# Attention and two expert layers in one program: sums, inversion and division of the last two attention halves placed one to three expert steps later

## The chip, the core and the metric

The program runs on one core of a Trainium2 chip. The metric is the device time of one execution in microseconds (us); the time before is the median of three runs. TensorE is called PE here, its weight loads PEld, VectorE DVE, ScalarE ACT, GpSimd POOL, and SP is the engine whose queue issues nearly all DMAs.

## What is computed

A clustered attention (queries see only the keys of their own cluster) feeds two feed-forward layers; the second one ends with a product with a cosine.

```
mask = q_assign[:, :, :, None] == k_assign[:, :, None, :]
scores = np.where(mask, scale * np.matmul(q, k.transpose(0, 1, 3, 2)), -1000000000.0)
attn = np.exp(scores - np.max(scores, axis=-1, keepdims=True))
attn = attn / (np.sum(attn, axis=-1, keepdims=True) + 1e-09)
x = np.matmul(attn, v)            # batch 2, heads 8, tokens 768, head size 64
x = transpose(0, 2, 1, 3) of x, as 1536 tokens x 512
h = np.maximum(x @ w_in, 0.0);  x = h * h @ w_out        # 512 -> 2048 -> 512
h = x @ w_in2;  out = (h * np.cos(h)) @ w_out2           # 512 -> 2048 -> 512
```

All inputs and the output are float32. The matrix products of the two layers are made of three products of split operands (a high and a low part).

## The kernel before, in words

**Attention.** The 16 heads of the two batches are 8 pairs of heads. The 768 queries of a pair are two halves of 384, so there are 16 halves, numbered 0 to 15; the last two are 14 (`last`) and 15 (`end`). A half has six units of scores, one per 128 keys: `scores` (L454, PE into one of three two-bank `unit` tiles), `exponent` (L464, ACT), `add_up` (L476, POOL, which adds the six exponentials into `acc`), and `pv` (L484, PE, the product with v into `o_ps[0]`, three units at a time).

**What ends a half.** `move_out` (L535, ACT) copies the product out of `o_ps[0]`; `sums` (L499, eight small matmuls on PE) adds `acc` over the keys into the bank `o_ps[1]`; `move_sums` (L506, ACT) copies them out of it; `deal_sums` (L513, a DMA of SP) spreads them over 128 partitions; `invert` (L517, DVE) takes reciprocals; `store_inverse` (L523 or L525) and `load_inverse` (L531, two DMAs) bring them back as rows over 64 partitions each; `divide` (L538, DVE) multiplies; `combine_high` (L559, ACT) and `combine_low` (L563, POOL) write the result's high and low parts into `xh` and `xl`, the input of the first layer.

**Expert steps.** `moe` walks over steps 0, 1, 2, ...: a step is one block of 512 tokens and one group of 128 hidden units. Step i makes `h_mm(i)` (L674, twelve matmuls into one bank), then its elementwise work (`ew_first`: L689, L690, L691 on ACT; `ew_last`: L712, on POOL in the first steps), and `y_mm(i-2)` (L727, twelve matmuls). The banks of `h_mm` turn in a ring of four from step 2 on; two of the four are `o_ps[0]`, which step 3 takes, and `o_ps[1]`, which step 5 takes. Block 0 (steps 0 to 7) needs halves of the first batch only; steps 8 to 15 (block 1) read what half 14 writes, steps 16 on (block 2) what half 15 writes.

**Weights.** Each half of a weight group (`w_f_0` for `h_mm`, `w_f_1` for `y_mm`) is loaded by SP (`w_load`, L118) and split by `w_split`: six DVE instructions (L143, L144, L145, L146, L147, L139) and one cast on ACT (L138), which reads what L146 writes. `split_some` puts a share of these into each step. `load_mid` issues six such loads, `load_late` eight; the latter need the memory of the attention's tiles.

**What sets the order.** Every engine runs its instructions in the order in which the program writes them. During attention the order is a sorted list of due times (the tables `finish` and `places`); in the expert steps it is the text of `moe`, with hooks: functions that are called in step i right after `h_mm(i)`, before the elementwise work and the `y_mm` of that step. For half 14 `sums`, `move_sums`, `deal_sums` and `invert` stand in the table, and the rest in hooks 0 and 2; half 15 has all after `move_out` in hooks 3 and 5, with the division not dealt over partitions (its reciprocal works on `r` itself).

Of the kernel before, what the change touches and what calls it, by code (L numbers as in the profile page):

```python
# [38 lines left out]
def tile_kernel(ctx: ExitStack, tc: tile.TileContext, q, k, v, centroids, w1i, w1o, w2i, w2o, out):  # L39
# [69 lines left out]
    def w_load(m, f, hs=(0, 1)):  # L109
        wi, wo = ((w1i, w1o), (w2i, w2o))[m]  # L110
        for h in hs:
            raw_ = wraw[m, f, h] = chunk(f, h, U32, f"wraw{m}_")
            if h == 0:
                raw_ = raw_.rearrange("p (a c) -> p a c", a=KD)
                src = wi.bitcast(U32)[:, f * 2 * P : (f + 1) * 2 * P].rearrange("(a p) c -> p a c", p=P)
            else:
                src = wo.bitcast(U32)[f * P : (f + 1) * P, :]
            nc.sync.dma_start(raw_, src)  # L118
# [49 lines left out]
    NU = NPAIR * SP  # L168
# [8 lines left out]
    def small():  # L177
        return free_small.pop(0)

    def give_small(u):  # L180
        free_small.append(u)
# [259 lines left out]
    last = 2 * NPAIR - 2  # L441
# [25 lines left out]
    def add_up(u_):  # L467
        hb, kt = divmod(u_, NT)
        if kt == 0:
            return  # L470
        assert u_ not in unread and u_ - 1 not in unread
        if kt == 1:
            accs[hb] = ap.tile([P, 2, HALF], F32, tag="acc", name=f"acc{hb}", bufs=2)
        a = ptiles[u_ - 1] if kt == 1 else accs[hb]
        for j in range(2):
            nc.gpsimd.tensor_tensor(accs[hb][:, j], a[:, j], ptiles[u_][:, j], ALU.add)  # L476

    def pv(u_):
        n, c = divmod(u_, SP)
        hf, kt = divmod(c, NT)  # L480
        t = ptiles[u_]
        assert u_ not in unread
        for j in range(2):
            nc.tensor.matmul(  # L484
                o_ps[0][j * D : (j + 1) * D, :HALF], lhsT=raw[n, "v"][:, kt, j, :], rhs=t[:, j],
                start=(kt == 0), stop=(kt == NT - 1),
            )
# [5 lines left out]
    def sums(hb):  # L493
        su[hb] = u = small()
        a = accs.pop(hb)
        for j in range(2):
            for h in range(2):
                g = R * (2 * j + h)
                nc.tensor.matmul(  # L499
                    u[g : g + R, 0, :QH], lhsT=ones[:, :R], rhs=a[:, j, h * QH : (h + 1) * QH], start=True, stop=True  # L500
                )

    def move_sums(hb):
        u = su.pop(hb)
        r = inv[hb] = ap.tile([P, QH], F32, tag="r", name=f"r{hb}", bufs=2)
        nc.scalar.activation(r, u[:, 0, :QH], AF.Identity, bias=eps)  # L506
        give_small(u)


    def deal_sums(hb):  # L510
        r = inv.pop(hb)
        t = inv[hb] = ap.tile([P, 2 * HALF // P], F32, tag="dealt", name=f"dealt{hb}", bufs=2)
        nc.sync.dma_start(t, r[0:P:R])  # L513

    def invert(hb):
        r = inv[hb]
        nc.vector.reciprocal(r, r)  # L517

    def store_inverse(hb):
        r = inv.pop(hb)  # L520
        row = rows_[hb] = dram.tile([2, HALF], F32, tag="row", name=f"row{hb}", bufs=2)
        if r.shape[1] == QH:
            nc.sync.dma_start(row.rearrange("j (h c) -> (j h) c", h=2), r[0:P:R])  # L523
        else:
            nc.sync.dma_start(row.rearrange("j (a c) -> (j a) c", c=r.shape[1]), r)  # L525

    def load_inverse(hb):
        row = rows_.pop(hb)
        rb = rbs[hb] = ap.tile([P, HALF], F32, tag="rb", name=f"rb{hb}", bufs=2)
        for j in range(2):  # L530
            nc.sync.dma_start(rb[j * D : (j + 1) * D], row[j : j + 1, :].broadcast_to([D, HALF]))  # L531

    def move_out(hb):
        x = xs[hb] = ap.tile([P, HALF], F32, tag="x", name=f"x{hb}", bufs=3)
        nc.scalar.copy(x, o_ps[0][:, :HALF])  # L535

    def divide(hb):
        nc.vector.tensor_tensor(xs[hb], xs[hb], rbs.pop(hb), ALU.mult)  # L538

    def combine(hb):  # L540
        combine_high(hb)
        combine_low(hb)
# [14 lines left out]
    def combine_high(hb):  # L557
        for src, dst, low in parts_of(hb):
            nc.scalar.copy(dst, src)  # L559

    def combine_low(hb):
        for src, dst, low in parts_of(hb):
            nc.gpsimd.tensor_tensor(low, src, dst.bitcast(F32), ALU.subtract)  # L563
        xs.pop(hb)
# [248 lines left out]
    def load(m, f, h, at):  # L813
        w_load(m, f, (h,))
        ready[m, f, h] = at
# [19 lines left out]
    def moe(hooks):  # L835
        phs = {}
        for idx in range(n_steps + LAG):
            fresh = idx < n_steps
            yi = idx - LAG
            end = yi in closes  # L840
            for i in (idx, idx + 1) if idx == n_steps - 2 else (idx,):
                if i < n_steps and i not in phs:
                    phs[i] = h_mm(i)
                    loads_h(i)
                    if steps[i][0] == 1:
                        ew_zero(i, phs[i])
            for f in hooks.get(idx, ()):
                f()
            two = 0 <= idx - 1 < n_steps and steps[idx - 1][0] == 1
            if two:  # L850
                ew_mid(idx - 1, phs[idx - 1])
                by_pool = idx - 1 < n0 + 16
                if end or by_pool:
                    ew_last(idx - 1, nc.gpsimd if by_pool else nc.vector)
            if end:
                y_mm(yi)
                y_out(yi)
            if fresh:
                ew_first(idx, phs[idx])
                if steps[idx][0] == 0 and idx < FA:  # L860
                    ew_last(idx, nc.gpsimd)
            if two and not (end or by_pool):
                ew_last(idx - 1, nc.vector)
            split_some(idx, 12)
            if fresh and steps[idx][0] == 0 and idx >= FA:
                ew_last(idx, nc.vector)
            if yi >= 0:
                if not end:
                    y_mm(yi)
                loads_y(yi)  # L870
        assert not pending and not owed and not splitting
# [130 lines left out]
        (17.431, combine_high),  # L1002
        (18.530, combine_low),
    ]
    ending = sums, move_sums, deal_sums, invert, move_out

    SCORES, EXPS, SMAX, LARGEST = (0.000, -0.982, -0.808, -1.110, -3.572, -3.690), (0.016, -0.428, -0.788, -0.613, -3.224, -3.681), (-2.502, -5.046, -2.335, -1.548, -2.669, -0.447), (-0.170, -4.189, -2.105, -1.354, -2.566, 0.314)
    ADD, PV, WEIGHTS, WARMTH = 1.481, -1.548, 0.96, 0.97
# [31 lines left out]
        (pv, 89): 89.454, (move_out, 14): 89.482, (invert, 13): 89.676, (scores, 90): 90.000,  # L1040
        (exponent, 90): 90.016, (scores, 91): 90.018, (scores, 94): 90.428, (combine_low, 12): 90.531,
        (exponent, 91): 90.572, (exponent, 94): 90.776, (store_inverse, 13): 91.168, (scores, 92): 91.192,
        (exponent, 92): 91.212, (scores, 95): 91.310, (exponent, 95): 91.319, (sums, 14): 91.408,
        (move_sums, 14): 91.869, (scores, 93): 91.890, (load_inverse, 13): 92.298, (exponent, 93): 92.387,
        (pv, 90): 92.452, (pv, 91): 92.453, (pv, 92): 92.454, (divide, 13): 94.260,
        (deal_sums, 14): 94.761, (combine_high, 13): 95.431, (invert, 14): 95.676, (combine_low, 13): 96.531,
    }
    own_places = {key[0] for key in places}
    steps_ = []
# [1 line left out]
    def at(when, f, *a):  # L1051
        steps_.append((places.get((f, *a[-2:]) if f in own_places else None, when), len(steps_), f, a))
# [32 lines left out]
        for r, f in finish:  # L1085
            at(NT * hb + r, f, hb)
    for r, f in finish:
        if f in ending:
            at(NT * last + r, f, last)
    for g in range(-LEAD, NU):  # L1090
        c = g % len(SMAX)
# [30 lines left out]
    def load_late():  # L1122
        att.close()
        late = ctx.enter_context(tc.tile_pool(name="late", bufs=1, reuse_waits="tile"))
        for f, h in wanted[n_early + n_mid :]:
            home[f, h] = late, f"l{f}_{h}"
            if (f, h) not in STAGE:
                load(0, f, h, 6)

    open_banks()  # L1130
    end = last + 1
    moe({
        0: [lambda: store_inverse(last), lambda: load_inverse(last)],
        1: [
            lambda: add_up(NU - 3), lambda: add_up(NU - 2),
            *(lambda u_=u_: pv(u_) for u_ in range(NU - GROUP, NU)), lambda: move_out(end),
        ],
        2: [
            lambda: add_up(NU - 1), lambda: divide(last), lambda: combine(last), load_mid,
        ],  # L1140
        3: [
            lambda: sums(end), lambda: move_sums(end), lambda: invert(end),
            lambda: store_inverse(end), lambda: load_inverse(end),
        ],
        5: [lambda: divide(end), lambda: combine(end), load_late],
    })


# [26 lines left out]
```

## Time and profile before

| | before |
|---|---|
| median of 3 runs | 771.99 us (771.91 to 772.01) |
| the profiled execution, its own time | 772.14 us |
| its span in the trace | 770.4 us |
| PE busy | 753.0 us (98%) |
| DVE busy | 582.2 us (76%) |
| ACT busy | 360.9 us (47%) |
| POOL busy | 252.6 us (33%) |
| mean granted PE clock | 0.996 |

A busy share is an average over the whole span; the stretch that the change touches lies between 228 and 300 us, where attention ends and the expert steps begin. The 1.7 us between the span and the execution's time lie outside the trace.

### The profile page before, as it was taken

The numbers are of one execution on the slowest core, as the hardware profiler recorded it, in microseconds if no ns is written. First come the engines' busy times: TensorE is split into PE (matmuls) and PEld (weight loads), VectorE is DVE, ScalarE is ACT, GpSimd is POOL, SyncE is SP. The second block draws the span as 40 slices with busy tenths as digits, with TensorE's granted clock in tenths as the row PEclk, the third lists the DMA queues.
The fourth block names the chain that finished last, engine by engine and source line by source line (L and its number), as shares of the span: only waits on it lengthen the run. The fifth ranks groups of instructions, "written<-read, shape, count | busy, mean of one in ns | idle before, by whom it ended". The sixth has DMA issues, their size and how long they took to land.

```text
span 770.4 us, 11398 instructions
## 1 busy us (share of the span) xinstructions
PE 753.0 (98%) x4259; PEld 583.6 (76%) x4259; DVE 582.2 (76%) x922; ACT 360.9 (47%) x609; POOL 252.6 (33%) x267
## 2 busy tenths in 40 slices
PE   6999999999999999999999999999999999999997
PEld 4667676675656787888888888888887888888886
DVE  3857887878899999969784118779999866666665
ACT  3456666574654445453444435353343433333332
POOL 8597889889998520000000000012222000000000
PEclk8999999999999999999999999999999999999999
DMA  4554445333516451067300006630000100010001
GB/s 115 134 148 121 112 125 138 86 86 83 158 49 195 156 199 56 0 199 239 109 1 1 0 28 196 203 107 15 0 1 0 56 1 1 0 55 1 0 1 54
DMA packets 76763, 62.21 MB, mean 81 GB/s; under 512 B 45472, under 2 KB 68004, under 8 KB 76708
## 3 DMA queue, kind: packets, MB, share of 16 engines
q1 hardware_dynamic: 75044, 61.00, 26.7%
q8 instruction: 33, 0.54, 0.3%
q10 hardware_dynamic: 1664, 0.49, 0.3%
q14 instruction: 22, 0.18, 0.1%
HBM read 48.27 MB, written 5.29 MB: 70 GB/s over the span
## 4 chain that ended last, share of the span: by engine, by line
PE 70%; issue 12%; DVE 11%; POOL 5%; DMA 1%; ACT 0%; POOLq 0%; SPq 0%; DVEq 0%; ACTq 0%
PE bank L727 25%; PE o_ps L674 12%; PE bank L674 12%; PE unit L454 7%; PE o_ps L484 6%; PE unit L387 4%; POOL ewr L712 3%; DVE top L146 2%; DVE m L397 2%; DVE top L145 1%; DVE w L139 1%; DVE aux L143 1%; DVE aux L144 1%; PE unit L247 1%; DVE aux L147 1%
## 5 line engine op out<-in xcount | busy, mean ns | idle before, releaser
L476 POOL TENSOR_TENSOR acc<-acc,p 128x384 f32<-128x384 f32 x128 | 142.9, 1147 | 3.3 <-ACT p L464 3.2
L727 PE MATMUL bank<-ewr,w 128*128 128x512 f32 x576 | 138.6, 389 | 0.6 <-DVE kept L755 0.6
L727 PE MATMUL bank<-w,ewr 128*128 128x512 f32 x576 | 138.7, 390 | 0.4 <-POOL ewr L712 0.4
L712 POOL TENSOR_TENSOR ewr<-ews,ewr 128x512 fp32r<-128x512 f32 x24 | 31.9, 1328 | 301.1 <-ACT ewr L708 288.3
L674 PE MATMUL bank<-xh,w 128*128 128x512 f32 x392 | 128.8, 390 | 0.0
L727 PEld LDWEIGHTS bank<-w,ewr 128*128 128x128 f32 x576 | 107.7, 188 | 24.1 <-ACT ewr L708 1.1
L727 PEld LDWEIGHTS bank<-ewr,w 128*128 128x128 f32 x576 | 108.0, 188 | 23.6 <-ACT ewr L691 1.0
L397 DVE TENSOR_REDUCE m<-unit 128x2 f32<-128x768 f32 x96 | 90.2, 949 | 44.5 <-PE unit L387 40.5
L674 PE MATMUL o_ps<-xh,w 128*128 128x512 f32 x376 | 123.4, 389 | 0.0
L712 DVE TENSOR_TENSOR ewr<-ews,ewr 128x512 fp32r<-128x512 f32 x72 | 49.5, 688 | 53.0 <-ACT ewr L691 48.4
L674 PEld LDWEIGHTS bank<-xh,w 128*128 128x128 f32 x392 | 73.6, 188 | 16.5 <-issue 0.6
L464 ACT ACTIVATE p<-unit 128x768 f32<-128x768 f32 x96 | 72.1, 814 | 22.9 <-PE unit L454 22.6
L699 ACT ACTIVATE ews<-ews,narrow_t 128x512 f32<-128x512 f32 x48 | 34.8, 726 | 100.3 <-DVE ews L698 100.3
L674 PEld LDWEIGHTS o_ps<-xh,w 128*128 128x128 f32 x376 | 70.6, 188 | 14.7
L674 PE MATMUL bank<-xl,w 128*128 128x512 f32 x196 | 76.3, 389 | 0.0
L674 PE MATMUL o_ps<-xl,w 128*128 128x512 f32 x188 | 73.1, 389 | 0.0
L484 PE MATMUL o_ps<-p,rawv 128*64 128x384 f32 x384 | 68.5, 494 | 0.0
L454 PE MATMUL unit<-set,set 64*128 64x384 f32 x512 | 64.6, 338 | 1.7 <-DVE m L397 1.7
L138 ACT CAST w<-top 128x512 fp32r<-128x512 f32 x64 | 39.3, 617 | 35.8 <-DVE top L146 35.7
L139 DVE SCALAR_TENSOR_TENSOR w<-aux,aux 128x512 fp32r<-128x512 f32 x64 | 51.7, 808 | 1.9
L693 DVE TENSOR_SCALAR ews<-ews 128x512 f32<-128x512 f32 x48 | 20.3, 423 | 42.3 <-ACT ews L703 42.2
L146 DVE SCALAR_TENSOR_TENSOR top<-wraw,top 128x512 uint32<-128x512 uint32 x64 | 50.1, 782 | 1.5
(124 smaller groups left out, 1072.1 us busy)
## 6 DMA issues: line engine op xcount, KB each, us to landing
wraw<-in_moe_w_in_dram SPq DMA_DIRECT2D x32, 512.0 KB
wraw<-in_moe_w_out_dram SPq DMA_DIRECT2D x32, 512.0 KB
ext<-set SPq DMA_DIRECT2D x32, 96.0 KB
rawv<-in_v_dram SPq DMA_DIRECT2D x8, 384.0 KB
rb<-row SPq DMA_DIRECT2D x32, 96.0 KB
rawq<-in_q_dram SPq DMA_DIRECT2D x7, 384.0 KB
rawk<-in_k_dram SPq DMA_DIRECT2D x7, 384.0 KB
held<-kept SPq DMA_DIRECT2D x8, 256.0 KB
```

The costliest lines, as they stand in the source:

```text
L138: nc.scalar.copy(w[:, 0], top.bitcast(F32))
L139: ve.scalar_tensor_tensor(w[:, 1], restf, 2.0**-20, power.bitcast(F32), ALU.mult, ALU.mult)
L146: cost(690, lambda: ve.scalar_tensor_tensor(top, high, 0xC0000000, top, ALU.bitwise_and, ALU.bitwise_or)),
L397: nc.vector.tensor_reduce(d["m"][:, i, :, kh], u[:, :, :HALF], AX, ALU.max)
L454: nc.tensor.matmul(u[:, j, :HALF], lhsT=a[r], rhs=b[r, qs], start=(p == 0), stop=(p == len(ops) - 1))
L464: nc.scalar.activation(t, u[:, :, :HALF], AF.Exp, scale=SCALE)
L476: nc.gpsimd.tensor_tensor(accs[hb][:, j], a[:, j], ptiles[u_][:, j], ALU.add)
L484: nc.tensor.matmul(o_ps[0][j * D : (j + 1) * D, :HALF], lhsT=raw[n, "v"][:, kt, j, :], rhs=t[:, j], start=(kt == 0), stop=(kt == NT - 1),)
L674: nc.tensor.matmul(ph, lhsT=w[:, a, :], rhs=x[blk][:, a, :], start=(a == i == 0), stop=(a == KD - 1 and i == 2))
L699: nc.scalar.activation(e2, e2, AF.Sin, bias=hpi)
L712: e.tensor_tensor(al, e2, ah.bitcast(F32), ALU.subtract)
L727: nc.tensor.matmul(y, lhsT=a, rhs=b, start=(idx in opens and i == 0), stop=(idx in closes and i == 2))
```

## The change

`sums`, `move_sums` and `deal_sums` of half 14 leave the table of due times and go to hook 1, in front of the last `pv`; its `invert` goes to hook 2, with `store_inverse` and `load_inverse` (before: hook 0), and its `divide` and `combine` go from hook 2 to hook 4. Half 15 goes from hook 3 to hook 4 with its `sums` and `move_sums` and now has `deal_sums` as the others; its `invert` with the store and load goes to hook 5, its `divide`, `combine` and `load_late` go to hook 7. The weights of `load_late` may be split from step 9 on, not from step 6.

```diff
-    ending = sums, move_sums, deal_sums, invert, move_out
 ...
-        (exponent, 92): 91.212, (scores, 95): 91.310, (exponent, 95): 91.319, (sums, 14): 91.408,
+        (exponent, 92): 91.212, (scores, 95): 91.310, (exponent, 95): 91.319,
 ...
     for r, f in finish:
-        if f in ending:
+        if f is move_out:
             at(NT * last + r, f, last)
 ...
             if (f, h) not in STAGE:
-                load(0, f, h, 6)
+                load(0, f, h, 9)
 ...
     moe({
-        0: [lambda: store_inverse(last), lambda: load_inverse(last)],
         1: [
+            lambda: sums(last), lambda: move_sums(last), lambda: deal_sums(last),
             lambda: add_up(NU - 3), lambda: add_up(NU - 2),
             *(lambda u_=u_: pv(u_) for u_ in range(NU - GROUP, NU)), lambda: move_out(end),
         ],
-        2: [
-            lambda: add_up(NU - 1), lambda: divide(last), lambda: combine(last), load_mid,
+        2: [lambda: add_up(NU - 1), lambda: invert(last), lambda: store_inverse(last), lambda: load_inverse(last), load_mid],
+        4: [
+            lambda: divide(last), lambda: combine(last),
+            lambda: sums(end), lambda: move_sums(end), lambda: deal_sums(end),
         ],
-        3: [
-            lambda: sums(end), lambda: move_sums(end), lambda: invert(end),
-            lambda: store_inverse(end), lambda: load_inverse(end),
-        ],
-        5: [lambda: divide(end), lambda: combine(end), load_late],
+        5: [lambda: invert(end), lambda: store_inverse(end), lambda: load_inverse(end)],
+        7: [lambda: divide(end), lambda: combine(end), load_late],
     })
```

How the instructions then stand on the engines, at three places. The numbers behind a name tell tiles apart and differ between the two programs.

PE, the end of attention, before: `acc_2909` is the sum of half 14, `p_2953` to `p_2995` are the first three exponentials of half 15, and `bank_3073` with `w_0_0` is `h_mm(0)`.

```order
L454 MATMUL unit_71<-set_2_111 128x384 x2
L499 MATMUL o_ps_66<-acc_2909,ones 32x192 x4
L454 MATMUL unit_70<-set_0_109,set_1_110 128x384 x2
L454 MATMUL unit_70<-set_0_109,set_3_112 128x384 x2
L454 MATMUL unit_70<-ext_0_119,ext_1_120 128x384 x2
L454 MATMUL unit_70<-set_2_111,set_1_110 128x384 x2
L484 MATMUL o_ps_65<-p_2953,rawv_2784 64x384 x2
L484 MATMUL o_ps_65<-p_2975,rawv_2784 64x384 x2
L484 MATMUL o_ps_65<-p_2995,rawv_2784 64x384 x2
L674 MATMUL bank_3073<-xh_90,w_0_0_884 128x512
```

PE, the same sums now; the first three rows are the end of `h_mm(1)`.

```order
L674 MATMUL bank_3063<-xh_90,w_1_0_1241 128x512 x2
L674 MATMUL bank_3063<-xl_93,w_1_0_1241 128x512
L674 MATMUL bank_3063<-xh_90,w_1_0_1241 128x512
L499 MATMUL o_ps_66<-acc_2909,ones 32x192 x4
L484 MATMUL o_ps_65<-p_3022,rawv_2784 64x384 x2
L484 MATMUL o_ps_65<-p_2977,rawv_2784 64x384 x2
L484 MATMUL o_ps_65<-p_3005,rawv_2784 64x384 x2
L674 MATMUL bank_3064<-xh_90,w_2_0_1596 128x512
```

The sums of half 14 moved behind two `h_mm`, six matmuls of `pv` and the last scores. Those of half 15 (`acc_3036`, now `acc_3030`) moved in the same way, from between `h_mm(3)` and `y_mm(1)` to between `h_mm(4)` and `y_mm(2)`; the next matmuls into their bank `o_ps_66` are `h_mm(5)`, which follows `y_mm(2)` in both programs.

ACT in the steps 2 to 4, before: `x_2940` is half 14, `r_3210` the sums of half 15; `bank_3073`, `o_ps_65` and `bank_3074` are the banks of `h_mm(2)`, `h_mm(3)` and `h_mm(4)`.

```order
L138 CAST w_4_1_3133<-top_208 128x512
L559 CAST xh_91<-x_2940 128x256
L559 CAST xh_92<-x_2940 128x128
L689 ACTIVATE ews<-bank_3073 128x512
L690 ACTIVATE ews<-ews 128x512
L691 CAST ewr<-ews 128x512
L138 CAST w_7_0_3176<-top_207 128x512
L506 ACTIVATE r_3210<-o_ps_66,eps 128x192
L689 ACTIVATE ews<-o_ps_65 128x512
```

ACT now: `r_3247` is the sums of half 15, and `bank_3065` is the bank of `h_mm(4)`.

```order
L138 CAST w_7_0_3171<-top_207 128x512
L689 ACTIVATE ews<-o_ps_65 128x512
L690 ACTIVATE ews<-ews 128x512
L691 CAST ewr<-ews 128x512
L138 CAST w_5_1_3207<-top_208 128x512
L559 CAST xh_91<-x_2940 128x256
L559 CAST xh_92<-x_2940 128x128
L506 ACTIVATE r_3247<-o_ps_66,eps 128x192
L689 ACTIVATE ews<-bank_3065 128x512
```

The copy of the sums of half 15 (L506) stood behind the cast of `w_7_0`; it now stands behind the elementwise work of step 3, the cast of `w_5_1` and the two casts of half 14 (L559).

DVE, the division of half 14 (L538), before.

```order
L139 SCALAR_TENSOR_TENSOR w_4_1_3133<-aux_206,aux_205 128x512
L143 TENSOR_SCALAR aux_206<-wraw_7_0_3039 128x512
L144 SCALAR_TENSOR_TENSOR aux_206<-wraw_7_0_3039,aux_206 128x512
L538 TENSOR_TENSOR x_2940<-x_2940,rb_3089 128x384
L145 TENSOR_SCALAR top_207<-wraw_7_0_3039 128x512
```

DVE, the same division now.

```order
L139 SCALAR_TENSOR_TENSOR w_5_1_3207<-aux_206,aux_205 128x512
L143 TENSOR_SCALAR aux_206<-wraw_6_1_3046 128x512
L144 SCALAR_TENSOR_TENSOR aux_206<-wraw_6_1_3046,aux_206 128x512
L145 TENSOR_SCALAR top_207<-wraw_6_1_3046 128x512
L146 SCALAR_TENSOR_TENSOR top_207<-wraw_6_1_3046,top_207 128x512
L538 TENSOR_TENSOR x_2940<-x_2940,rb_3149 128x384
```

Between L139 of `w_4_1` and the division stood two instructions of the split of `w_7_0`; now the whole splits of `w_7_0` and `w_5_1`, four instructions of that of `w_6_1` and the reciprocal of half 14 stand there, 17 in all. That reciprocal stood ahead of `w_4_1` before; the reciprocal of half 15, which stood in the split of `w_5_1`, is now behind the division.

## Rows read from the trace of the kernel before

**Rows 1.** The page, busy time of each engine (share of the span) and instructions.
```profile
PE 753.0 (98%) x4259; PEld 583.6 (76%) x4259; DVE 582.2 (76%) x922; ACT 360.9 (47%) x609; POOL 252.6 (33%) x267
```

**Rows 2.** Waits of PE, 228 to 300 us: total, times, longest.
```profile
PE o_ps L499 <- POOL acc L476: 2.8, 4, 0.9
```

**Rows 3.** Timeline of PE: start, length, line, times, idle before and releaser.
```profile
231.88 0.52 PE L499 MATMUL o_ps<-acc,ones 128*32 128x192 f32 x4 [0.44 <-POOL acc L476]
...
233.74 0.61 PE L454 MATMUL unit<-set,set 64*128 64x384 f32 x4
...
247.11 0.39 PE L674 MATMUL bank<-xh,w 128*128 128x512 f32 x1
...
253.78 0.52 PE L499 MATMUL o_ps<-acc,ones 128*32 128x192 f32 x4 [0.84 <-POOL acc L476]
...
255.36 3.03 PE L727 MATMUL bank<-ewr,w 128*128 128x512 f32 x12
...
263.67 0.39 PE L674 MATMUL o_ps<-xh,w 128*128 128x512 f32 x1
...
294.33 3.01 PE L727 MATMUL bank<-ewr,w 128*128 128x512 f32 x12 [0.57 <-DVE kept L755]
```

**Rows 4.** Windows of PE: stretch, length, busy (instructions), granted clock, DMA share, GB/s.
```profile
300.00:500.00 200.00, 200.00 (x884) 1.00 0.29 93
```

**Rows 5.** Timeline of POOL.
```profile
252.28 2.58 POOL L476 TENSOR_TENSOR acc<-acc,p 128x384 f32<-128x384 f32 x2
...
266.79 1.29 POOL L712 TENSOR_TENSOR ewr<-ews,ewr 128x512 fp32r<-128x512 f32 x1 [3.24 <-issue]
```

**Rows 6.** Timeline of ACT.
```profile
257.10 0.61 ACT L559 CAST xh<-x 128x256 fp32r<-128x256 f32 x2 [3.58 <-DVE x L538]
257.62 0.59 ACT L689 ACTIVATE ews<-bank 128x512 f32<-128x512 f32 x1
...
259.95 0.42 ACT L506 ACTIVATE r<-o_ps,eps 128x192 f32<-128x192 f32 x1
```

**Rows 7.** Timeline of DVE.
```profile
255.44 0.43 DVE L143 TENSOR_SCALAR aux<-wraw 128x512 uint32<-128x512 uint32 x1
...
256.52 0.55 DVE L538 TENSOR_TENSOR x<-x,rb 128x384 f32<-128x384 f32 x1
...
265.41 0.43 DVE L143 TENSOR_SCALAR aux<-wraw 128x512 uint32<-128x512 uint32 x1
...
266.94 1.69 DVE L146 SCALAR_TENSOR_TENSOR top<-wraw,top 128x512 uint32<-128x512 uint32 x1
...
269.85 0.43 DVE L143 TENSOR_SCALAR aux<-wraw 128x512 uint32<-128x512 uint32 x1
...
272.10 0.43 DVE L147 TENSOR_SCALAR aux<-top 128x512 uint32<-128x512 uint32 x1
272.44 0.55 DVE L538 TENSOR_TENSOR x<-x,rb 128x384 f32<-128x384 f32 x1
...
273.63 1.29 DVE L143 TENSOR_SCALAR aux<-wraw 128x512 uint32<-128x512 uint32 x1
```

**Rows 8.** Timeline of SP's DMA issues.
```profile
246.15 1.84 SPq L118 DMA_DIRECT2D wraw<-in_moe_w_in_dram  x3
...
263.67 0.55 SPq L523 DMA_DIRECT2D row<-r  x1
265.32 1.10 SPq L531 DMA_DIRECT2D rb<-row  x2
```

**Rows 9.** Windows of PE at the kernel's start, columns as in Rows 4.
```profile
8.00:13.80 5.80, 3.31 (x22) 0.98 0.60 136
13.80:16.10 2.30, 1.31 (x7) 0.50 0.44 113
16.10:20.40 4.30, 4.25 (x19) 0.50 0.58 140
20.40:22.00 1.60, 1.60 (x15) 1.00 1.25 284
```

More of the change, by code (lines that the diff above doesn't have):

```diff
@@ L1042, in tile_kernel @@
         (exponent, 91): 90.572, (exponent, 94): 90.776, (store_inverse, 13): 91.168, (scores, 92): 91.192,
-        (exponent, 92): 91.212, (scores, 95): 91.310, (exponent, 95): 91.319, (sums, 14): 91.408,
-        (move_sums, 14): 91.869, (scores, 93): 91.890, (load_inverse, 13): 92.298, (exponent, 93): 92.387,
+        (exponent, 92): 91.212, (scores, 95): 91.310, (exponent, 95): 91.319,
+        (scores, 93): 91.890, (load_inverse, 13): 92.298, (exponent, 93): 92.387,
         (pv, 90): 92.452, (pv, 91): 92.453, (pv, 92): 92.454, (divide, 13): 94.260,
-        (deal_sums, 14): 94.761, (combine_high, 13): 95.431, (invert, 14): 95.676, (combine_low, 13): 96.531,
+        (combine_high, 13): 95.431, (combine_low, 13): 96.531,
     }
```

## The prediction

> **What bounds the kernel now.** I read the page's busy shares first: PE works 98% of the span and no other engine more than 76% [rows 1]. So the time is PE's work plus PE's waits, and I look only for what adds or removes a wait of PE. The waits of PE between 228 and 300 us come next: the one the change aims at is the sums (L499) waiting for POOL's additions, four times, 2.8 us in all [rows 2]. In PE's timeline the two halves stand apart: the sums of half 14 begin at 231.88 and the next scores at 233.74; those of half 15 begin at 253.78 and `y_mm(1)` follows at 255.36 [rows 3]. After that PE has one more wait, 0.57 us at 294.33 for DVE [rows 3], and from 300 to 500 us it is busy for all 200.00 us [rows 4]. What PE loses or gains before 300 us therefore moves the end by as much.
>
> The third view is the other engines' place in the program at the same moment. ACT's L689 at 257.62 is the elementwise work of step 2, whose last matmul began at 247.11 [rows 3, 6]. It had nothing to wait for but its place behind L559, which itself had been idle 3.58 us for the division on DVE (256.52 for 0.55 us) [rows 6, 7]. So around step 3 ACT is ten us behind PE, and what holds ACT is DVE, which works off weight splits without a gap. That lag costs nothing as long as PE reads nothing that stands late in ACT's row.
>
> **The change, part by part.**
>
> *Sums of half 14, two `h_mm` later.* POOL has finished their input long before the new place, so the wait goes. From 231.88 to 233.74 are 1.86 us, with 0.44 of idle time before: 2.30. The eight small matmuls still have to run; two groups that overlap take about the length of one, 0.52 us [rows 3]. Gain 1.8 us.
>
> *Sums of half 15, one `h_mm` and one `y_mm` later.* 253.78 to 255.36 are 1.58 us, with 0.84 before: 2.42, less 0.52, so 1.9 us [rows 3]. The last additions of POOL end at 252.28 + 2.58 = 254.86 [rows 5]; the new place comes, with the first gain and `y_mm(1)` and `h_mm(4)` ahead of it, at about 257, so nothing of this wait stays. Together PE would reach `h_mm(5)`, which began at 263.67 [rows 3], at 263.67 − 3.7 = 260.0.
>
> *What now stands in front of `h_mm(5)`.* It writes the bank `o_ps[1]`, out of which ACT's L506 must first have copied the sums of half 15. Before, L506 ran at 259.95 [rows 6], 3.3 us ahead of need (260.37 against 263.67). Now it stands behind both L559 of half 14, and they behind the division, for which DVE first has to do 17 instructions instead of 2 after the split of `w_4_1`. I follow that row. DVE began the split of `w_7_0` at 255.44 [rows 7]; what stands ahead is the same but for one reciprocal of six elements, which returns a few instructions later, so 255.44 holds for the sum of both. A whole split with a POOL subtraction beside it took 265.41 to 269.85 = 4.44 us, with its L146 at 1.69 us [rows 7] while POOL ran L712 from 266.79 for 1.29 us [rows 5]. The next split, up to 273.63 and less the division in it (0.55), took 3.23 us [rows 7]. Two subtractions of POOL fall into this stretch, those of steps 2 and 3, whose elementwise work ACT now does directly behind the casts of `w_4_1` and `w_7_0`. So: 255.44 + 4.44 + 4.44 = 264.3; four instructions of `w_6_1`, as 269.85 to 272.10 = 2.25 [rows 7]; the division 0.55: 267.1. ACT's two casts take 257.62 − 257.10 = 0.52 and L506 0.42 [rows 6]: 268.1. PE would wait from 260.0 to 268.1, 8.1 us, and `y_mm(3)`, whose operands would be ready, stands behind `h_mm(5)` in PE's row and waits with it. Against 263.67 that is **4.4 us later**. Bounds: with no POOL op beside the two splits 255.44 + 2 × 3.23 + 2.25 + 0.55 + 0.94 = 265.6, 2.0 us later; with a third one 1.2 more, 269.3, 5.6 us later. I take 268.1, since both subtractions follow on casts that DVE itself times.
>
> The Trainium skill, "SBUF — State Buffer", Who interferes with whom, says that DVE and GpSimd hold a shared port pair exclusively and that the later one blocks for the other's whole instruction. By that rule two ops of 1.29 us would cost DVE 2.6 us where the rows give 2 × 1.2, so `h_mm(5)` would start 0.2 us later; where DVE starts first it would lose nothing, which is the lower bound. The trace agrees within that.
>
> *The clock.* A PE wait this long does not occur in the trace of before; the nearest row is the start. There PE worked 3.31 of 5.80 us from 8.00 on, and from 13.8 the granted clock was 0.50 (1.2 instead of 2.4 GHz). It stayed there through 2.30 us with 1.31 us of work and 4.30 us with 4.25 us of work, and was 1.00 from 20.40 on [rows 9]. After 8.1 us with no matmul at all I expect the same: the first 4.3 us of work at half speed, a loss of **2.15 us**. Bounds: 0 if the clock stays up, and 3.3 us if the whole 6.6 us (2.30 + 4.30) fall on work.
>
> The Trainium skill, "TensorE: Matmul & The Clock Gate", HAM oscillation, says that an idle wait lets the clock drop and that each restart is cold; a rule against this change, and it points to the same term.
>
> *The wait at 294.33.* It is DVE being late with the copies of the first block. DVE's row up to there is hardly changed while PE arrives over 6 us later, so DVE is there first: **−0.57 us**.
>
> *DMAs.* `deal_sums`, store and load of half 14 now stand ahead of `load_mid` in SP's queue, and the store waits for a reciprocal at about 256.8. Half 15's way before shows the price: store at 263.67, load at 265.32, and the division at 272.44 did not wait for it, so at most 7.1 us from issue to use [rows 7, 8]. The load would be issued at 258.7 and be there by 265.8 at the latest, ahead of the division (266.6). `load_mid`, issued from 246.15 before [rows 8], comes some 14 us later, around 260; DVE reads the first of these weights at 273.63 before [rows 7], and PE not ahead of step 24, so this and the later `load_late` cost nothing. If that cover failed, DVE would wait behind the division, not in front of it. The added `deal_sums` of half 15 shortens its reciprocal and lies behind the division too. POOL's subtractions move by one place and are waited for by nobody before step 4.
>
> **Sum** against the profiled execution: 772.14 + 4.4 + 2.15 − 0.57 = 778.1 us. The median of before is 0.15 lower than that execution, so 778.0.
>
> **Rivals.**
> *The waits simply go (faster).* If ACT reaches L506 of half 15 before 260.0, nothing holds `h_mm(5)`, and 772.0 − 3.7 = 768.3. For it: this is just what L506 did before (259.95), and the four waits are real. It decides at the division: DVE would have to reach it by about 258.5, 8 us sooner than I reckon, and 17 instructions can't be done in the 3 us from 255.44. Even at the lower bound PE waits over 5 us.
> *A draw.* The same gate opens at about 263.7, the new wait eats the gain: 772. It needs DVE 2 us faster than with no POOL op beside it.
> *The wait without the clock.* 772.0 + 4.4 − 0.57 = 775.8, if PE's clock survives 8 us of rest. Against it stands the start, where sparse work was enough for the fall.
> *More than I count.* A third POOL op and the long stretch of slow clock: 772.0 + 5.6 + 3.3 − 0.57 = 780.3.
>
> **How the numbers follow.** Forecast 778.0 with a chance of 0.71; clock stays up 0.11; more than I count 0.08; draw 0.05; faster 0.05. The range leaves out the two last cases and half of the upper one: 774.6 (the lower bound of the gate with some loss by the clock, 772.0 + 2.0 − 0.57 + about 1.2) to 780.3. A measurement of this kernel tells about 0.2% (1.5 us) from no change; slower by more has the three first cases, 0.90.
>
> **What would show it.** In the trace of after: no wait of L499 for POOL; one wait of PE before L674 into `o_ps`, seven to nine us long, released by ACT's L506, at 260 to 268; on ACT L559 idle for DVE's L538 right ahead of L506; a granted clock of 0.50 for some four us after it; no wait at the first L727 after the first block. I am wrong if L506 of half 15 runs before 260, if the division on DVE comes clearly before 265, or if the clock stays at 1.00 after the wait.

## The result

The changed kernel takes **778.12 us** (median of 4 runs, 777.01 to 778.33), the kernel before 772.00 beside it. The ratio is 1.0072, with a 95% interval of 1.0060 to 1.0084: slower by 6.1 us. Its profiled execution took 778.33 us with a span of 776.6, against 772.14 and 770.4 of before.

The busy times of the page hardly differ from [rows 1]: PE has the same work (753.1 us, 4259 instructions) in a longer span.

The waits of PE from 215 to 310 us (total, times, longest), to hold against [rows 2]:

```profile
PE o_ps L674 <- ACT r L506: 8.0, 1, 8.0
PE unit L454 <- DVE m L397: 1.3, 1, 1.3
PE o_ps L484 <- ACT p L464: 0.2, 1, 0.2
```

The four waits for POOL, 2.8 us, are gone, as is the one for DVE at the first block's end. In their place stands one wait of 8.0 us for ACT's copy of the sums of half 15. PE's timeline shows where (start, length, idle before and releaser as in [rows 3]):

```profile
240.37 0.53 PE L499 MATMUL o_ps<-acc,ones 128*32 128x192 f32 x8
...
256.74 0.53 PE L499 MATMUL o_ps<-acc,ones 128*32 128x192 f32 x8
257.21 3.02 PE L727 MATMUL bank<-ewr,w 128*128 128x512 f32 x12
268.24 0.79 PE L674 MATMUL o_ps<-xh,w 128*128 128x512 f32 x1 [8.01 <-ACT r L506]
...
273.52 3.10 PE L727 MATMUL bank<-ewr,w 128*128 128x512 f32 x12
276.46 0.39 PE L674 MATMUL bank<-xh,w 128*128 128x512 f32 x1
```

In the kernel before, `y_mm(2)` and `y_mm(3)` stand here:

```profile
260.95 2.88 PE L727 MATMUL bank<-ewr,w 128*128 128x512 f32 x12
...
266.39 2.88 PE L727 MATMUL bank<-ewr,w 128*128 128x512 f32 x12
```

Both groups of sums now run through without a wait, and `y_mm(2)` starts at 257.21 instead of 260.95: PE is 3.7 us ahead of before. Then `h_mm(5)` starts at 268.24, 4.57 us behind [rows 3], and takes 5.28 us to the next start (268.24 to 273.52) instead of 2.72 in before (263.67 to 266.39). What PE waited for stands in ACT's timeline, which answers to [rows 6]:

```profile
263.35 0.62 ACT L138 CAST w<-top 128x512 fp32r<-128x512 f32 x1 [1.96 <-DVE top L146]
267.26 0.60 ACT L559 CAST xh<-x 128x256 fp32r<-128x256 f32 x2 [3.29 <-DVE x L538]
267.77 0.41 ACT L506 ACTIVATE r<-o_ps,eps 128x192 f32<-128x192 f32 x1
```

The input of L506 was there from 257.3 on. It was read ten us later, since L506 stands behind the cast of `w_5_1`, for which ACT idled 1.96 us, and the two casts of half 14, for which it idled 3.29 us. Both times it idled for DVE. DVE, which answers to [rows 7], did not idle itself:

```profile
255.57 1.50 DVE L143 TENSOR_SCALAR aux<-wraw 128x512 uint32<-128x512 uint32 x1
...
260.15 0.43 DVE L143 TENSOR_SCALAR aux<-wraw 128x512 uint32<-128x512 uint32 x1
...
261.68 1.63 DVE L146 SCALAR_TENSOR_TENSOR top<-wraw,top 128x512 uint32<-128x512 uint32 x1
...
264.54 0.43 DVE L143 TENSOR_SCALAR aux<-wraw 128x512 uint32<-128x512 uint32 x1
...
266.67 0.55 DVE L538 TENSOR_TENSOR x<-x,rb 128x384 f32<-128x384 f32 x1
```

The splits of `w_7_0` and `w_5_1` start at 255.57 and 260.15, that of `w_6_1` at 264.54, and only behind its fourth instruction comes the division of half 14.

The windows of PE (stretch, length, busy with instructions, granted clock, DMA share, GB/s, as in [rows 4, 9]) show the second half of the loss:

```profile
259.80:264.00 4.20, 0.43 (x2) 0.96 0.42 93
264.00:268.00 4.00, 0.00 (x0) 0.50 1.05 358
268.00:270.00 2.00, 1.76 (x4) 0.50 1.03 395
270.00:272.00 2.00, 2.00 (x6) 0.50 0.93 356
272.00:274.00 2.00, 2.00 (x7) 0.53 0.08 10
274.00:276.00 2.00, 2.00 (x10) 1.00 0.08 9
```

The clock fell to 0.50 (1.2 GHz) during the wait and was back at 1.00 only at about 273.9, after 5.7 us of work. From 300 to 500 us PE is busy for all 200.00 us, as in [rows 4].

### The profile page after: what moved, and what is told of

It is laid out like the page before. It is cut to its first block, busy times and chain, and to the rows that moved or that the text cites. A ratio compares the mean times of both kernels' runs of the same rounds, so it can differ in the third digit from the quotient of the medians.

```text
span 776.6 us, 11399 instructions
## 1 busy us (share of the span) xinstructions
PE 753.1 (97%) x4259; PEld 584.5 (75%) x4259; DVE 582.3 (75%) x922; ACT 360.4 (46%) x609; POOL 253.0 (33%) x267
## 4 chain that ended last, share of the span: by engine, by line
PE 73%; issue 11%; DVE 7%; POOL 5%; DMA 1%; ACT 1%; SPq 0%; POOLq 0%; DVEq 0%; ACTq 0%
PE bank L727 27%; PE o_ps L674 13%; PE bank L674 13%; PE unit L454 7%; PE o_ps L484 6%; PE unit L387 4%; POOL ewr L712 3%; DVE m L397 2%; PE unit L247 1%; POOL set L273 1%; DVE top L145 1%; DMA wraw<-in_moe_w_out_dram 1%; DVE top L146 1%; DVE aux L144 1%; DVE w L139 1%
## 5 line engine op out<-in xcount | busy, mean ns | idle before, releaser
L674 PE MATMUL o_ps<-xh,w 128*128 128x512 f32 x376 | 125.3, 395 | 8.0 <-ACT r L506 8.0
L712 POOL TENSOR_TENSOR ewr<-ews,ewr 128x512 fp32r<-128x512 f32 x24 | 32.3, 1344 | 309.2 <-ACT ewr L708 292.7
L712 DVE TENSOR_TENSOR ewr<-ews,ewr 128x512 fp32r<-128x512 f32 x72 | 49.5, 688 | 55.8 <-ACT ewr L691 51.2
L484 PE MATMUL o_ps<-p,rawv 128*64 128x384 f32 x384 | 68.8, 494 | 0.2 <-ACT p L464 0.2
L454 PE MATMUL unit<-set,set 64*128 64x384 f32 x512 | 64.6, 338 | 1.7 <-DVE m L397 1.7
L139 DVE SCALAR_TENSOR_TENSOR w<-aux,aux 128x512 fp32r<-128x512 f32 x64 | 52.5, 820 | 1.9
L146 DVE SCALAR_TENSOR_TENSOR top<-wraw,top 128x512 uint32<-128x512 uint32 x64 | 49.7, 777 | 1.5
L144 DVE SCALAR_TENSOR_TENSOR aux<-wraw,aux 128x512 f32<-128x512 uint32 x64 | 49.1, 768 | 1.6
```

Source lines behind the costliest of these rows:

```text
L139: ve.scalar_tensor_tensor(w[:, 1], restf, 2.0**-20, power.bitcast(F32), ALU.mult, ALU.mult)
L144: cost(690, lambda: ve.scalar_tensor_tensor(restf, low, 2.0**-32, rest, ALU.mult, ALU.add)),
L146: cost(690, lambda: ve.scalar_tensor_tensor(top, high, 0xC0000000, top, ALU.bitwise_and, ALU.bitwise_or)),
L454: nc.tensor.matmul(u[:, j, :HALF], lhsT=a[r], rhs=b[r, qs], start=(p == 0), stop=(p == len(ops) - 1))
L484: nc.tensor.matmul(o_ps[0][j * D : (j + 1) * D, :HALF], lhsT=raw[n, "v"][:, kt, j, :], rhs=t[:, j], start=(kt == 0), stop=(kt == NT - 1),)
L674: nc.tensor.matmul(ph, lhsT=w[:, a, :], rhs=x[blk][:, a, :], start=(a == i == 0), stop=(a == KD - 1 and i == 2))
```

## The experiments

Each time stands beside the kernel before on the same chip: 772.17 us for the first four, 772.08 us for the other four.

**The copy of the sums ahead of the division.** One hook is turned round, so that on ACT L506 no longer stands behind L559. DVE's row stays as it is.

```diff
         4: [
-            lambda: divide(last), lambda: combine(last),
             lambda: sums(end), lambda: move_sums(end), lambda: deal_sums(end),
+            lambda: divide(last), lambda: combine(last),
         ],
```

> The changed kernel with the order inside hook 4 turned round: sums, move_sums and deal_sums of half 15 first, then divide and combine of half 14. Theory (ACT's copy of the sums stands behind the casts of half 14, which wait for the division on DVE): the copy now stands only behind the cast of w_5_1, which ended at about 264.0 in the changed kernel's trace, so h_mm(5) begins near 264.4 instead of 268.2, PE waits about 4.2 us, and without a fall of the clock the time is 772.0 + 0.7 - 0.6 = 772.1; with a fall as long as in the changed kernel 2.8 more, 774.9. Rival (the wait hangs on the DMAs of half 14 or on the weight loads that now stand behind them on SP): the order on ACT changes nothing, PE waits 8 us and the time stays 778.

Measured: **774.03 us**, ratio 1.0021 (1.0007 to 1.0034), 4.1 us less than the changed kernel. PE's timeline and, below it, ACT's:

```profile
264.26 0.80 PE L674 MATMUL o_ps<-xh,w 128*128 128x512 f32 x1 [4.13 <-ACT r L506]
```

```profile
263.27 0.62 ACT L138 CAST w<-top 128x512 fp32r<-128x512 f32 x1 [1.95 <-DVE top L146]
263.80 0.41 ACT L506 ACTIVATE r<-o_ps,eps 128x192 f32<-128x192 f32 x1
267.18 0.60 ACT L559 CAST xh<-x 128x256 fp32r<-128x256 f32 x2 [2.97 <-DVE x L538]
```

The division still ends near 267, and PE no longer cares. So the division was the last gate in front of L506, worth 4 us; the one behind it is the cast of `w_5_1`. `h_mm(5)` took 264.26 to 269.28 = 5.02 us, 2.3 us over its usual 2.72, by the clock again.

**Another bank for `h_mm(5)`.** The ring is turned, so that step 5 writes `banks[0]`, and `o_ps[1]` is due one step later. Nothing else changes.

```diff
-        ph = banks[(idx - 2) % 4] if idx > 1 else (banks[0], y_banks[3])[idx]
+        if idx < 2:
+            ph = (banks[0], y_banks[3])[idx]
+        else:
+            ph = banks[idx - 2] if idx < 5 else banks[(0, 3, 1, 2)[(idx - 5) % 4]]
```

> The changed kernel, but the ring of banks is turned by one from step 5 on: h_mm(5) takes the bank that step 2 had, and o_ps[1], the bank of the sums, comes to h_mm(6). Theory (the wait is for this bank alone): h_mm(5) begins at 260.1 without a wait, h_mm(6) would begin at 265.6 and waits to 268.2, 2.6 us, the clock stays up, and against h_mm(6) of before (269.11) PE is 0.9 us ahead, with the 0.6 us wait behind the first block gone: 770.5. Rival (PE would wait at this point for something else that is late on DVE or ACT, the operands of y_mm(3) or the weights): the wait stays near 8 us in all and the time near 778.

Measured: **771.86 us**, ratio 0.9997 (0.9988 to 1.0007). PE's timeline (the lines of the program are three further down):

```profile
260.01 0.39 PE L677 MATMUL bank<-xh,w 128*128 128x512 f32 x1
...
268.19 0.50 PE L677 MATMUL o_ps<-xh,w 128*128 128x512 f32 x1 [2.58 <-ACT r L506]
...
272.64 2.69 PE L730 MATMUL bank<-ewr,w 128*128 128x512 f32 x11
```

`h_mm(5)` starts at 260.01, without a wait: PE was held by the bank and not by its operands. The wait moved to `h_mm(6)` and shrank by one `h_mm` and one `y_mm`, from 8.0 to 2.6 us. The clock fell after this short rest too: `h_mm(6)` took 268.19 to 272.64 = 4.45 us instead of 2.72.

The time is 1.4 us over what was expected, and the clock is only the smaller part of that. At the end of the first block PE meets DVE again: `y_mm(8)`, the first product of the next block, needs the banks that DVE (L755 in before, L758 here) and ACT copy out. DVE's line in before, and below it in this run:

```profile
293.49 1.28 DVE L755 COPY kept<-bank 128x512 f32<-128x512 f32 x2
```

```profile
293.19 1.28 DVE L758 COPY kept<-bank 128x512 f32<-128x512 f32 x2
```

In before PE waited for these copies, and `y_mm(8)` began 0.84 us after the first of them (294.33 [rows 3]). Here it began at 294.43 without a wait, but it could not have begun before about 293.19 + 0.84 = 294.0, however early PE came (an estimate from these rows). So of the 1.7 us of the clock about 0.4 reached the end, and the other 1.0 us of the miss is this second gate, which the expectation left out.

**PE kept busy through the wait.** 34 matmuls whose result nothing reads stand ahead of `h_mm(5)`.

```diff
+            if idx == 5:
+                for _ in range(34):
+                    nc.tensor.matmul(
+                        banks[0], lhsT=wsplit[0, 4, 0][:, 0, :P], rhs=xh[0][:, 0, :], start=True, stop=True
+                    )
```

> The changed kernel with 34 matmuls of 128x512 ahead of h_mm(5), into the bank that step 6 overwrites; their result is not used. They take 34 x 0.227 = 7.7 us of the 8.0 us in which PE waits. Theory (of the 6.1 us lost some 2.8 are a fallen clock): h_mm(5) begins at 268.2 as in the changed kernel, the granted clock stays 1.00, and the time is 778.1 - 2.8 = 775.3. Rival (the clock costs nothing, the whole loss is the wait): 778.1.

Measured: **775.87 us**, ratio 1.0052 (1.0036 to 1.0069). A window of PE, and its timeline:

```profile
265.00:270.00 5.00, 4.65 (x21) 1.00 1.06 383
```

```profile
260.03 7.87 PE L843 MATMUL bank<-xh,w 128*128 128x512 f32 x34
268.25 0.50 PE L674 MATMUL o_ps<-xh,w 128*128 128x512 f32 x1 [0.35 <-ACT r L506]
...
271.11 2.88 PE L727 MATMUL bank<-ewr,w 128*128 128x512 f32 x12
```

`h_mm(5)` starts at the same moment as in the changed kernel, and the clock stays at 1.00. The DMA engines are as busy as there (a share of 1.06 here, 1.05 and 1.03 there), so the fall came with the rest and not with the weight loads that ran at the same time. The clock alone is therefore worth 778.12 − 775.87 = 2.25 us by the medians, and 2.6 by the two spans (776.6 and 774.0).

**Half 14 alone.** Half 14 as in the change; half 15 with `sums` to `load_inverse` in hook 3 and its division in hook 5, as before, and `load_late` ready at 6.

```diff
-                load(0, f, h, 9)
+                load(0, f, h, 6)
 ...
-        4: [
-            lambda: divide(last), lambda: combine(last),
-            lambda: sums(end), lambda: move_sums(end), lambda: deal_sums(end),
+        3: [
+            lambda: sums(end), lambda: move_sums(end), lambda: invert(end),
+            lambda: store_inverse(end), lambda: load_inverse(end),
         ],
-        5: [lambda: invert(end), lambda: store_inverse(end), lambda: load_inverse(end)],
-        7: [lambda: divide(end), lambda: combine(end), load_late],
+        4: [lambda: divide(last), lambda: combine(last)],
+        5: [lambda: divide(end), lambda: combine(end), load_late],
```

> Half 14 as in the change (sums in hook 1, inversion in hook 2, division in hook 4), half 15 as in the kernel before (hooks 3 and 5, not dealt). Theory: PE reaches the sums of half 15 1.8 us sooner and waits there that much longer, since POOL's additions still end at 254.9; the copy out of the bank stands behind the cast of w_7_0 as before (about 260), so h_mm(5) begins near 263.7 as before: 772.0, within 0.5, no long wait and no fall of the clock. Rival (each half's move is worth its own wait): 770.2. Rival (the loss comes from half 14's later division and the weight loads behind it): 774 or more.

Measured: **775.94 us**, ratio 1.0056 (1.0037 to 1.0074), 3.9 us more than expected: a miss. Three pieces of PE's timeline:

```profile
253.68 0.52 PE L499 MATMUL o_ps<-acc,ones 128*32 128x192 f32 x4 [2.56 <-POOL acc L476]
254.82 0.52 PE L499 MATMUL o_ps<-acc,ones 128*32 128x192 f32 x4 [0.62 <-POOL acc L476]
255.27 4.57 PE L727 MATMUL bank<-ewr,w 128*128 128x512 f32 x12
...
298.04 2.32 PE L727 MATMUL bank<-ewr,w 128*128 128x512 f32 x9 [2.29 <-DVE kept L755]
```

The gain of half 14 was expected to go into a longer wait for POOL at the sums of half 15, and it did: `y_mm(1)` starts at 255.27, where it stood before ([rows 3], 255.36). Two things were not foreseen. After the rests of 2.56 and 0.62 us the clock fell, and `y_mm(1)` took 4.41 us to the next start instead of 2.87 in before (255.36 to 258.23). And DVE came late to the end of the first block, so that PE waited 2.29 us there instead of 0.57; DVE had idled for a DMA. SP's issues, and DVE's timeline:

```profile
265.69 0.56 SPq L523 DMA_DIRECT2D row<-r  x1
272.48 1.11 SPq L531 DMA_DIRECT2D rb<-row  x2
```

```profile
276.15 0.56 DVE L538 TENSOR_TENSOR x<-x,rb 128x384 f32<-128x384 f32 x1 [3.39 <-DMA rb<-row]
...
297.20 1.28 DVE L755 COPY kept<-bank 128x512 f32<-128x512 f32 x2
```

Here `load_mid` has moved behind half 14's load and its six loads run ahead of half 15's store. From store to load there are 6.8 us instead of 1.65 [rows 8]; the DMA share is 0.87 to 1.08 from 264 to 272 us and 0.07 from 272 to 274, so the load was issued when the weight loads had ended.

Only the second of the two reaches the end. The division of half 15 comes 3.71 us later than before (276.15 against 272.44 [rows 7]), DVE's copies 3.71 us later (297.20 against 293.49), and so does `y_mm(8)` (298.04 against 294.33). PE waits there for DVE; had the clock stayed up, it would have come sooner and waited longer. So the 3.9 us are the late DMA but for some tenths, and the 1.5 us of the clock are hidden in that wait.

**Half 15 alone.** Half 14 stays as before (its table entries and hooks 0 and 2); half 15 as in the change.

```diff
 ...
+        0: [lambda: store_inverse(last), lambda: load_inverse(last)],
         1: [
-            lambda: sums(last), lambda: move_sums(last), lambda: deal_sums(last),
 ...
-        2: [lambda: add_up(NU - 1), lambda: invert(last), lambda: store_inverse(last), lambda: load_inverse(last), load_mid],
-        4: [
-            lambda: divide(last), lambda: combine(last),
-            lambda: sums(end), lambda: move_sums(end), lambda: deal_sums(end),
+        2: [
+            lambda: add_up(NU - 1), lambda: divide(last), lambda: combine(last), load_mid,
         ],
+        4: [lambda: sums(end), lambda: move_sums(end), lambda: deal_sums(end)],
```

> Half 15 as in the change (sums in hook 4, dealt, inversion in hook 5, division in hook 7), half 14 as in the kernel before (table, hooks 0 and 2). Theory (what holds h_mm(5) is the place of the copy L506 in ACT's row): the copy stands behind the cast of w_5_1, but no longer behind casts of half 14; in DVE's row that is at about 263.5, the copy ends near 264.0, and PE, 1.9 us sooner by the wait saved, comes to h_mm(5) at 261.8 and waits 2.2 us. Before it was at 263.67, so +0.3, less the 0.6 at the first block's end: 771.9 with the clock up, and up to 1.7 more if 2.2 us of rest are enough for the clock to fall, as 2.6 were in the run with another bank: 773.4. Rival (half 15's move alone makes the loss): 776 or more, with a wait near 8 us.

Measured: **774.81 us**, ratio 1.0032 (1.0021 to 1.0043), above what was expected. PE's timeline and ACT's:

```profile
259.59 3.04 PE L727 MATMUL bank<-ewr,w 128*128 128x512 f32 x12 [0.79 <-ACT ewr L691]
265.09 0.79 PE L674 MATMUL o_ps<-xh,w 128*128 128x512 f32 x1 [2.47 <-ACT r L506]
```

```profile
264.10 0.62 ACT L138 CAST w<-top 128x512 fp32r<-128x512 f32 x1 [2.22 <-DVE top L146]
264.63 0.42 ACT L506 ACTIVATE r<-o_ps,eps 128x192 f32<-128x192 f32 x1
```

With the division out of its way, L506 still waits for the cast of `w_5_1`, as in the first experiment, and PE rests 2.47 us. ACT's elementwise work of step 2 shows up as a further gate, 0.79 us in front of `y_mm(2)`; it costs nothing here, since PE waits for L506 right behind it. `h_mm(5)` took 265.09 to 269.47 = 4.38 us: the clock again, 1.7 us. The copy had been reckoned 0.6 to 1.0 us too early.

**Fewer splits while the division is due.** The change as it is, but the steps 0 to 3 give less time to weight splits. The splits that are left out there follow later; the division of half 14 then has only four instructions of `w_7_0` behind `w_4_1` in front of it, not 17.

```diff
         if idx < n0:
-            return 2400 if idx < LAG else 3600
+            return 1500 if idx < 4 else 3600
```

> The changed kernel with one number more changed: in the steps 0 to 3 at most about four instructions of weight splits are put in a step (budget 1500 in place of 2400 and 3600); later steps take them. Theory (the wait is DVE's backlog in front of the division of half 14): the reciprocal of half 14 comes at about 253 in place of 257.7, the division at about 259, as soon as its rows have landed, the copy of the sums of half 15 ends at 260.5, and h_mm(5) begins at 260.5 with a wait under 1 us and the clock up. Both saved waits (3.7 us) and the 0.6 us stay saved: 772.1 - 3.7 - 0.6 + 0.4 = 768.2. Rival (the later places themselves cost time through the DMAs or through weights that are split too late): 772 or more.

Measured: **768.58 us**, ratio 0.9955 (0.9941 to 0.9968). ACT's timeline and DVE's:

```profile
260.12 0.60 ACT L559 CAST xh<-x 128x256 fp32r<-128x256 f32 x2 [4.80 <-DVE x L538]
260.64 0.41 ACT L506 ACTIVATE r<-o_ps,eps 128x192 f32<-128x192 f32 x1
```

```profile
259.54 0.55 DVE L538 TENSOR_TENSOR x<-x,rb 128x384 f32<-128x384 f32 x1
...
287.19 1.46 DVE L755 COPY kept<-bank 128x512 f32<-128x512 f32 x2
```

The copy runs 7.1 us sooner than in the changed kernel, PE waits 1.0 us instead of 8.0, the clock stays at 1.00, and 9.5 us are gone. Nothing further down the program pays for the postponed splits: behind 300 us PE waits once, 0.4 us, as in the changed kernel. The edit opens two gates at once: the division comes 7.1 us sooner, and DVE reaches its copies at the first block's end some 6 us sooner than in before (287.19 against 293.49). Without the second, `y_mm(8)` could not have begun before about 294.0, as in the run with the other bank, and nearly all of the gain would have been lost there. No run parts the two.

**The same with the kernel before**, to see what the splits are worth without the change; its edit is the same line.

> The kernel before with the same smaller share of splits in the steps 0 to 3 and nothing else. Theory: its waits for POOL's additions stay (2.8 us named, 3.7 with what hangs on them), since they do not hang on DVE; at most the 0.6 us behind the first block goes: 771.5 to 772.1. Rival (the smaller share is what brings the gain in the run with the changed kernel): 769 or less.

Measured: **771.35 us**, ratio 1.0003 (0.9991 to 1.0014). The wait at the first block's end is gone, as expected, and those for POOL stay: four of L499, 2.9 us in all.

**Both edits**: fewer splits, and the copy of the sums ahead of the division.

> The changed kernel with the smaller share of splits in the steps 0 to 3 and with the sums, move_sums and deal_sums of half 15 ahead of divide and combine of half 14 in hook 4. Theory: the copy of the sums then waits for nothing but the sums themselves and ends at about 257.7, before PE reaches h_mm(5) at 260.1: no wait there, 772.1 - 3.7 - 0.6 = 767.8, some tenths under the run without the turned order. Rival: as in that run, 772 or more.

Measured: **767.32 us**, ratio 0.9938 (0.9926 to 0.9950), 4.8 us under the kernel before and the fastest here. Of PE's waits from 215 to 310 us only the two small ones of the changed kernel are left (L454 for DVE, 1.3 us; L484 for ACT, 0.2). ACT's timeline:

```profile
257.24 0.42 ACT L506 ACTIVATE r<-o_ps,eps 128x192 f32<-128x192 f32 x1 [1.90 <-PE o_ps L499]
260.13 0.61 ACT L559 CAST xh<-x 128x256 fp32r<-128x256 f32 x2 [2.48 <-DVE x L538]
```

L506 now waits for PE instead of the other way round. The runs with one or the other edit side by side (us):

| | kernel before | the change | the change, copy ahead of the division |
|---|---|---|---|
| splits as they were | 772.0 | 778.12 | 774.03 |
| fewer in steps 0 to 3 | 771.35 | 768.58 | 767.32 |

With the splits thinned, the change is worth 771.35 − 768.58 = 2.8 us as it stands, and 771.35 − 767.32 = 4.0 us with the copy put first. In front of DVE's old row it costs 6.1.

## Why the prediction was right, step by step

The forecast was 778.0 us and slower; the time is 778.12. The mechanism is the one foretold, and each step can be held against a row.

*The gain of the sums.* Reckoned 1.8 + 1.9 = 3.7 us. `y_mm(2)` began 3.74 us sooner, and where nothing holds it `h_mm(5)` begins at 259.96 (both edits) or 260.01 (other bank): 260.0 was reckoned. But the two terms are not independent: half 14 alone gained 0.1 us at `y_mm(1)`, because POOL ends the sums of half 15 when it did before. In the whole change the second move takes that wait away, so the sum holds; that the first move is worth nothing by itself the prediction did not say. By parts, PE was 1.57 us ahead at `h_mm(3)` (248.49 against 250.06), where 1.8 were reckoned: a wait of 0.24 us for ACT's exponentials, in front of `pv`, is new. The other 2.17 came behind it, against 1.9.

*The gate.* Division at 266.6 to 267.1, end of L506 at 268.1, PE's wait 8.1, `h_mm(5)` 4.4 us later were reckoned; 266.67, 268.18, 8.01 and 4.57 came. The two splits took 4.58 and 4.39 us against 4.44 each, and the four instructions 2.13 against 2.25. One POOL subtraction fell beside each split, as reckoned. The first met L143 (1.50 instead of 0.43 us), the second L146 (1.63 instead of 0.69): 1.07 and 0.94 us of DVE for 1.29 and 1.30 of POOL, which began first both times (L712 at 255.50 and 261.47). The Trainium skill, "SBUF — State Buffer", Who interferes with whom, has the later of the two blocked for the other's whole instruction; the trace agrees within 0.4 us, and within 0.15 us of what POOL's instruction had left when DVE's began (1.22 and 1.09 us). That DVE's division is the gate is shown by the first and the sixth experiment, that it acts through the bank by the other bank.

*The clock.* This is the term that was **mis-sized**. 4.3 us of work at half speed were taken from the start [rows 9], so 2.15 us. The trace has `h_mm(5)` 2.56 us longer and `y_mm(3)` 0.22 longer (273.52 to 276.46 = 2.94 against 2.72), 2.8 us in all, over 5.7 us of work; by the busy PE it was 2.25 to 2.6 us. The first figure holds some 0.14 us that a restart costs with the clock up as well (`h_mm(5)` took 2.86 us with PE kept busy). All lie within the bounds of 0 to 3.3. The Trainium skill, "TensorE: Matmul & The Clock Gate", HAM oscillation, has each restart after such an idle wait cold, and the rows of the changed kernel agree: 0.50 from 264 to 272. After the shorter rests of 0.35 us (PE kept busy) and 0.99 us (fewer splits) the clock stayed at 1.00.

*The wait at 294.33.* Reckoned −0.57. It is gone. At the first block's end the shift against before goes from 7.35 us to 6.61, 0.74 less: PE's restart after the old wait had cost a little too, as that after 0.35 us does in the run with PE kept busy (268.25 to 271.11 = 2.86 instead of 2.72). What the prediction missed lies on the other side. It let every gain or loss of PE before 300 us move the end by as much. For a loss that holds, since PE then comes behind DVE's copies. A gain ends at them: DVE has no wait in front of its copies at 293.49, and the other bank shows the copies at 293.19 with the change in place.

*The DMAs.* Reckoned at nothing, with the cover named: half 14's load by 258.7, `load_mid` around 260. They were issued at 260.19 and 261.39, and the division at 266.67 did not wait. SP's issues:

```profile
260.19 1.11 SPq L531 DMA_DIRECT2D rb<-row  x2
261.39 1.64 SPq L118 DMA_DIRECT2D wraw<-in_moe_w_in_dram  x3
```

The load was 1.5 us later than reckoned, and by the 7.1 us that the prediction allowed it could have been there only at 267.3, behind the division. That bound was wide: in half 14 alone DVE waited for such a load, and from issue to use it took 3.7 us (272.48 to 276.15). The step holds for the whole change, but its reason is narrower than it was put: half 14 alone pays nearly all of its 3.9 us for this very move, since there half 15's store comes right behind the six loads.

*The sum.* 4.57 + 2.8 − 0.74 = 6.6 us stand at 301 us; reckoned were 6.0, and the time rose by 6.2 between the two profiled executions. Of the 0.4 us between, 0.12 go in `y_mm(8)` itself (the next start is 303.66 against 297.17, a shift of 6.49), 0.06 in small steps up to 755 us (6.43) and the rest behind it; where was not followed further. So the hit to 0.1 us is partly luck: the clock was reckoned 0.6 us too short, and small gains elsewhere made up for it.

*The rivals.* "The waits simply go" was priced at 768.3 and tied to the division being reached by about 258.5. With fewer splits the division came at 259.54 and the time was 768.58 with a wait of 1.0 us left. But the price left out DVE's copies at the first block's end, which the thinning brought forward as well: had only L506 come early and DVE's row stayed as it was, `y_mm(8)` would have begun at about 294.0 instead of 294.33, which is some tenths and not 3.7 us (an estimate, not run). "The wait without the clock", priced at 775.8, is the run with PE kept busy: 775.87.

## What to carry to other kernels

Before a producer is moved later, look at what stands ahead of its **reader's release** on every engine in between: here a 0.4 us copy that frees a bank stood behind casts that waited for 17 instructions of a third engine, and PE paid 8 us for it. Put copies that free a bank ahead of work that waits for a slower engine, and thin out the background work of that engine where the moved step needs it; with the thinning alone the move brought 2.8 us, with both 4.0. Price a rest of TensorE with the clock that it may cost. Where two moves wait for the same engine, do not count on the gain of one without the other. And before a gain or a loss is carried to the end, look for the next place where TensorE meets the slower engine: a gain can stop there, and a loss can vanish in a wait that is there anyway.

## What the runs showed of the chip

The clock fell more often than I had expected. After rests of about 2.5 us already, the next 4.4 us of work ran mostly at half speed. The rests and what followed, each from PE's timeline and the granted clock of its windows:

| rest of PE, us | kernel | next group of twelve, us (2.72 without a rest) | clock |
|---|---|---|---|
| 0.99 | fewer splits | 2.85 | stayed at 1.00 |
| 2.47 | half 15 alone | 4.38 | fell |
| 2.56 and 0.62 | half 14 alone | 4.41 | fell |
| 2.58 | other bank | 4.45 | fell |
| 4.13 | copy ahead of the division | 5.02 | fell |
| 8.01 | the change | 5.28, and 0.22 in the next | fell |

In the three runs with a rest of some 2.5 us the next twelve matmuls took 1.7 us more than without a rest. What of it reaches the end hangs on what follows: all of it with half 15 alone, about 0.4 us with the other bank, nothing with half 14 alone, where PE waits for DVE at the first block's end in any case. Nor does the fall always come in the rest itself. With the other bank it came some 0.6 us after PE had started again at 268.19 (windows of PE as above):

```profile
266.00:268.00 2.00, 0.00 (x0) 1.00 1.11 401
268.00:270.00 2.00, 1.81 (x5) 0.69 1.04 392
```

Even the rests at the sums of the kernel before may cost it: in the profiled run of that kernel with fewer splits (772.96 us) they were 0.84 and 0.75 us long, and `y_mm(1)` behind them took 4.44 us to the next start, while six of its ten runs lie 1.6 us lower, at 771.15 to 771.38. In the kernel before, with 0.84 and 0.62 us, the clock stayed at 1.00. What decides between these two was not tried.
